# A Trainium2 kernel's convolution backward with its complex products summed before one inverse matmul each, and with its opening, gradient stores, load chain and shift-kernel gradient rearranged

## The chip, the cores and the metric

The kernel runs on one core of one Trainium2 chip, in bf16 with float32 accumulation. A core has five engines, each with its own instruction stream: TensorE (PE in the profile; its weight loads are listed apart as PEld), VectorE (DVE), ScalarE (ACT), GpSimd (POOL) and SyncE (SP). They meet only through semaphores. Here SP and POOL serve above all as queues that issue DMA transfers: what is issued on one of them leaves in order. The metric is device microseconds of one execution, taken as the median over several runs.

## The reference

The kernel computes the forward pass and all gradients of a four-step residual network over a sequence of 2048 positions with 448 channels. The hidden width of the dense part is 1792.

```python
def _A_ref(q, k, v, shift_k, ssm_k, ssm_D):
    k_shift = sum over t of k_pad[:, t:t + S, :] * shift_k[:, ks - 1 - t]     # 4 taps
    kv = k_shift * v
    y_f = rfft(kv padded to 2 S) * rfft(ssm_k padded to 2 S)
    y = irfft(y_f)[:S] + kv * ssm_D
    return q * y

def _B_ref(x, w1, w2):
    return silu(x @ w1) @ w2

x = A_q
x = x + _A_ref(_layernorm(x), A_k, A_v, A_shift_k, A_ssm_k, A_ssm_D)
x = x + _B_ref(_layernorm(x), B_w1, B_w2)
x = x + _A_ref(_layernorm(x), A_k, A_v, A_shift_k, A_ssm_k, A_ssm_D)
x = x + _B_ref(_layernorm(x), B_w1, B_w2)
out, vjp = jax.vjp(all of the above, ...); grads = vjp(grad_out)
```

(The 4-tap sum is shortened here to one line.) Two layers share all weights. The part A of a layer multiplies the normalized input by y, which does not depend on x, so y is computed once and serves both layers. Nine results leave: the output and the gradients of A_q, A_k, A_v, A_shift_k, A_ssm_k, A_ssm_D, B_w1 and B_w2.

## The kernel before

**Three sections, one stream of matmuls.** `_ssm_prefix` computes y: the shift convolution, the long convolution as a Fourier transform in two matmul stages (first stage L207, a turn by TensorE L348, second stage L218), the products with the kernel's spectrum (L449 and L450), the inverse of the second stage (L227 and L228) and of the first (L467). It leaves both spectra in DRAM (`SPEC_d`, L156). `Main.run` (L689) does both layers, forward and backward. `_ssm_suffix` (L1023) takes the gradient of y back through the convolution. The order of instructions on TensorE in the last two sections is the one in which the program emits them (L189). The other engines' instructions are placed by the framework's scheduler, and DMAs go out in the order of their queue, SP or POOL.

**Main.** The sequence is cut into 4 chunks of 512 positions (index c), each passing through layers L = 0 and 1. `fwd0` and `fwd1` do the part A of a layer: layer norm (`_ln`, L253, whose scaled copy is L274) and the gate (L549) on VectorE. `T` transposes a [128, 4, 448] tile by TensorE in two steps of 8 transposes (`transp`, L513; ScalarE copies each out of PSUM). `H` (7 steps of 8 matmuls, L597) multiplies by w1; ScalarE makes `aT` by silu and later the slope `dT` (L612). `O` (8 half steps, L619) multiplies by w2 and VectorE adds to the residual `X` (L623). On the way back `G` (7 steps, L638) multiplies the turned gradient by w2 transposed, and `N` (8 half steps, L665) by w1 transposed, followed by the layer norm's backward on VectorE (`_ln_bwd`). Where the program interleaves, a string gives the order of the steps, one letter a step. It does so in the opening, before the loop over chunks:

```python
        weave("TTGGGGtGtGG", T=self.T(k.gb0, gT, GBLK), G=self.G(gT, gh2), t=self.T(self.n0[0][1], nT, NBLK))
...
        weave("OOOOOOTOTO", O=self.O(0, 0, aT), T=self.T(gb1, gT, GBLK))
```

There the G steps of layer 1 (they need only `grad_out`, as `gb0` for chunk 0 and `gb1` for chunk 1) stand between the forward steps. `gb1` is loaded on POOL's queue (L715), and `w1T` comes by a transposing DMA on SP's queue (L486).

**Weight gradients.** The gradients of w1 and w2 need, for each of 14 blocks of 128 hidden channels, a sum over all 2048 positions of both layers: products of `a` (the silu outputs) or `g` (gradients times slope) with full-length tiles `X`, `go`, `n1m`, `n3m`. `store` (L496) writes `a` and `g` to DRAM (`OP_d`). For a of both layers and g of layer 1 it first turns each half by two transposing DMAs into a buffer and stores that by two more; g of layer 0 is stored as it is, and turned by the load (L873). `Jobs` (L813) is the stream of these matmuls: `load` (L861) brings a block into a `dstat` tile, `mms` (L876) does 16 matmuls of 448 columns in steps of four, and `jobs.run(n)` puts the next n steps at the place in TensorE's order where it is called; `jobs.run(1000)` at the end does what is left. After the main section (`pool is None`) every second `dstat` tile comes from the `hd` buffers (L195), which the main section used for `x0c` and `n00`, and the others from three buffers that held slopes.

**The convolution's backward.** First stage of the gradient of y (L1043), turned by TensorE (L1068) into 7 tiles `Zg`. Then, for each of 7 passes (cp): `spectrum` (L1078) does the second stage of the next tile and has VectorE write `xsw`, the tile with its real and imaginary halves exchanged (L1088); `inverse` (L1091) multiplies the tile by two stored spectra, that of kv for the gradient of the long kernel and that of the long kernel for the gradient of kv, and transforms back. In a chunk of 1024 columns it does this for each of the two: VectorE makes `pa` = tile x spectrum and `pb` = exchanged tile x spectrum, and 16 matmuls (8 with each, two different constant matrices of `Gsb`) add them up in PSUM as `ps_v`, 28 times in all; then 3 steps of jobs. After each pass VectorE does an eighth of the part A backward of layer 0 (`APart.run`, L1004), with loads and a store on POOL's queue. `spec_load` (L1056) brings both spectra for a pass by two DMAs of 512 KB; two buffers (`kk_c`, `kk_d`) alternate.

**The end.** gkv (L1142) gives the gradients of v and of the shifted k (`gks`), gK (L1162) the long kernel's. The shift kernel's gradient is the diagonal of a [channel x channel] product for each of four taps: for each of four blocks of 112 channels, 16 matmuls with 4 x 112 columns into `ps_sk` (L1174), of which VectorE keeps the diagonal by multiplying with the identity (`skjunk`, L1177). The gradient of k is formed on VectorE alone in 16 groups (L1186 to L1189), the last part stored from POOL's queue. The rest of the jobs follows.

## Time and profile before

| what | value |
|---|---|
| median of 3 runs | 779.42 us (769.31, 779.42, 792.57) |
| profiled execution, own time | 767.89 us |
| its span, first to last instruction | 765.8 us |
| mean granted TensorE clock | 0.988 |

Busy time by stretch of the span, from the windows view:

| stretch (us) | what runs there | PE | DVE | ACT | DMA share |
|---|---|---|---|---|---|
| 0 to 101 | prefix | 84.2 | 73.0 | 75.1 | 0.81 |
| 101 to 164 | opening of the main section | 50.1 | 32.3 | 40.0 | 1.12 |
| 164 to 541 | main section | 364.2 | 228.6 | 250.4 | 0.70 |
| 541 to 575 | first stage of the backward, and jobs | 33.5 | 10.8 | 21.1 | 0.96 |
| 575 to 680 | turn and 7 passes of products and inverse, and jobs | 104.7 | 76.9 | 51.3 | 1.02 |
| 680 to 715 | gkv and gK, and jobs | 33.0 | 27.5 | 16.8 | 0.98 |
| 715 to 766 | shift kernel's gradient, gradient of k, last jobs | 46.6 | 26.9 | 4.3 | 0.62 |

How to read the lines that follow: a row of the timeline or of the chain is start, duration, engine, line, operation, output <- inputs, shape, type and count; in square brackets stands the idle time of that engine before it, and what released it. L879 means line 879 of the kernel as printed above. Busy time of TensorE counts matmuls whose ends are modelled, and pipelined matmuls overlap, so the pace of a run of matmuls is read from the starts of neighbouring runs rather than from the mean duration of one. The granted clock is TensorE's, 1.00 being full speed.

### The profile page before, as it was taken

The page shows a single profiled execution, that of the slowest core. Times are in us where ns is not written, and L with a number is a line of the kernel's source. Part 1 is how long each engine was busy: PE and PEld are TensorE (multiplying, and loading weights), DVE is VectorE, ACT ScalarE, POOL GpSimd, SP SyncE. Part 2 cuts the span into 40 slices and gives each one's busy share as a digit, 9 for nine tenths or more (in the row PEclk, how much of TensorE's full clock was granted, in tenths as well). Part 3 has the DMA queues.
Part 4 walks back from the last instruction along what each step waited for, and adds up shares of the span by engine and source line. Part 5 has one row for each costly group of instructions (what it writes and reads, how often), then busy time and mean ns, then how long its engine had stood idle before and what let it go on. Part 6 is the DMA issues. An engine that isn't in the chain of part 4 may idle for free.

```text
span 765.8 us, 12392 instructions
## 1 busy us (share of the span) xinstructions
PE 716.3 (94%) x4831; PEld 403.5 (53%) x4860; DVE 476.0 (62%) x1148; ACT 458.9 (60%) x579; POOL 125.5 (16%) x209
## 2 busy tenths in 40 slices
PE   6998789779999999999999999999799999989997
PEld 4976544335444444544445544544366666656653
DVE  4789841664686747866379524825058777659970
ACT  4878867668776877769677793133465445445200
POOL 1134310120011100111001000000312323242311
PEclk9999999989999999999999999999899999999999
DMA  9949799989963898149882597185999999889972
GB/s 320 261 150 293 274 154 118 224 224 224 212 157 133 197 253 221 61 140 208 213 189 76 156 232 289 29 238 169 358 258 296 253 337 287 229 268 383 218 183 78
DMA packets 186363, 163.91 MB, mean 214 GB/s; under 512 B 135490, under 2 KB 166338, under 8 KB 185152
## 3 DMA queue, kind: packets, MB, share of 16 engines
q1 hardware_dynamic: 171776, 106.61, 57.9%
q0 software_dynamic: 14064, 56.50, 22.7%
q8 instruction: 38, 0.62, 0.3%
q14 instruction: 21, 0.17, 0.1%
q10 hardware_dynamic: 464, 0.00, 0.0%
HBM read 66.18 MB, written 60.10 MB: 165 GB/s over the span
## 4 chain that ended last, share of the span: by engine, by line
PE 61%; ACT 12%; DMA 9%; issue 8%; DVE 7%; POOL 3%; POOLq 0%; SPq 0%; DVEq 0%; ACTq 0%
PE ps_d L879 11%; PE ps_h L597 11%; PE ps_n L665 10%; PE ps_g L638 9%; PE ps_o L619 6%; ACT dT L612 4%; DMA out_dram<-gK 2%; DMA kx_s<-in_A_k_dram 2%; PE ps_d L914 2%; PE ps_t L520 2%; PE ps_s L207 2%; PE ps_v L228 2%; PE ps_v L227 2%; ACT aT L600 1%; ACT nT L521 1%
## 5 line engine op out<-in xcount | busy, mean ns | idle before, releaser
L879 PEld LDWEIGHTS <-dstat 128*128 128x128 bf16 x800 | 76.6, 99 | 70.6 <-DMA dstat<-a_d 4.6
L597 PE MATMUL ps_h<-nT,w1sb 112*128 112x512 bf16 x448 | 104.5, 379 | 4.2 <-ACT dT L111 1.9
L638 PE MATMUL ps_g<-nT,w2T 128*128 128x512 bf16 x432 | 101.0, 384 | 1.5 <-ACT nT L521 0.7
L665 PE MATMUL ps_n<-w1T,ghT 128*128 128x448 bf16 x448 | 95.3, 353 | 1.8 <-DVE ghT L650 1.7
L619 PE MATMUL ps_o<-w2sb,aT 128*128 128x448 bf16 x448 | 88.8, 352 | 0.0
L648 ACT CAST ghT<-ps_g 128x1024 bf16<-128x1024 f32 (+1 forms) x68 | 54.5, 824 | 52.5 <-PE ps_g L638 51.0
L600 ACT ACTIVATE aT<-ps_h 128x1024 bf16<-128x1024 f32 (+1 forms) x72 | 58.4, 834 | 30.5 <-PE ps_h L597 29.8
L597 PEld LDWEIGHTS <-w1sb 112*128 112x128 bf16 x448 | 43.7, 98 | 57.0 <-issue 7.5
L638 PEld LDWEIGHTS <-w2T 128*128 128x128 bf16 x448 | 44.0, 99 | 51.7 <-issue 1.6
L805 DVE SCALAR_TENSOR_TENSOR lb_v<-lb_u,n 128x448 bf16<-128x448 bf16 x48 | 29.9, 624 | 64.0 <-ACT lb_u L669 63.6
L665 PEld LDWEIGHTS <-ghT 128*128 128x128 bf16 x448 | 43.2, 98 | 44.3 <-DVE ghT L650 4.0
L619 PEld LDWEIGHTS <-aT 128*128 128x128 bf16 x448 | 43.4, 98 | 39.8
L612 ACT ACTIVATE dT<-dT 128x1024 bf16<-128x1024 bf16 (+1 forms) x64 | 54.6, 935 | 0.1
L267 POOL TENSOR_TENSOR rstd<-ln_ve,mhalf 128x2 f32<-128x2 f32 (+1 forms) x25 | 22.3, 890 | 187.6 <-DVE ln_ve L265 186.8
L111 ACT CAST dT<-ps_h 128x1024 bf16<-128x1024 f32 (+1 forms) x59 | 52.2, 902 | 0.0
L879 PE MATMUL ps_d<-n1m,dstat 128*128 128x448 bf16 x224 | 48.5, 356 | 0.1
L521 ACT COPY nT<-ps_t 128x1024 bf16<-128x1024 bf16 (+1 forms) x32 | 32.3, 1010 | 27.0 <-PE ps_t L520 27.0
L879 PE MATMUL ps_d<-n3m,dstat 128*128 128x448 bf16 x224 | 48.2, 352 | 0.2
L227 PE MATMUL ps_v<-Gsb,pa 128*128 128x128 bf16 x336 | 43.0, 219 | 3.1 <-DVE pa L449 3.0
L228 PE MATMUL ps_v<-Gsb,pb 128*128 128x128 bf16 x336 | 42.2, 219 | 2.3 <-DVE pb L450 1.9
L879 PE MATMUL ps_d<-X,dstat 128*128 128x448 bf16 x176 | 39.7, 366 | 4.2 <-DMA dstat<-a_d 4.2
L669 ACT ACTIVATE lb_u<-ps_n,rstd 128x448 bf16<-128x448 f32 x32 | 20.6, 645 | 32.2 <-PE ps_n L665 18.1
(197 smaller groups left out, 1201.2 us busy)
## 6 DMA issues: line engine op xcount, KB each, us to landing
dstat<-a_d SPq DMA_DIRECT2D x26, 512.0 KB, 5.7
a_d<-turned SPq DMA_DIRECT2D x16, 512.0 KB, 4.0
g_d<-ghT SPq DMA_DIRECT2D x8, 896.0 KB, 4.4
dstat<-g_d SPq DMA_DIRECT2D x14, 512.0 KB, 5.8
a_d<-turned SPq DMA_DIRECT2D x16, 384.0 KB, 3.2
N_d<-n POOLq DMA_DIRECT2D x11, 448.0 KB, 5.0
g_d<-turned SPq DMA_DIRECT2D x8, 512.0 KB, 3.4
spec_K<-Z POOLq DMA_DIRECT2D x7, 512.0 KB, 7.3
```

The lines of the kernel that those rows point to most:

```text
L111: nc.scalar.copy(out, in_)
L227: nc.tensor.matmul(pv[:, i, :], lhsT=pa[:, i * P:(i + 1) * P], rhs=k.Gsb[:, ga, :], start=True, stop=False)
L228: nc.tensor.matmul(pv[:, i, :], lhsT=pb[:, i * P:(i + 1) * P], rhs=k.Gsb[:, gb, :], start=False, stop=True)
L521: nc.scalar.copy(dst[:rows, 2 * h:2 * h + 2, :], pt[:rows])
L597: nc.tensor.matmul(ps[:, u, :], lhsT=self.w1sb[:, dc, ft * P:(ft + 1) * P], rhs=nT[:DC, dc, :], start=(dc == 0), stop=(dc == ND - 1))
L600: self.last_silu = nc.scalar.activation(aT[hh][:, o:o + hi - lo, :], ps[:, lo:hi, :], ACT.Silu)
L612: self.nc.scalar.activation(d[:, o:o + n, :], d[:, o:o + n, :], ACT.Derivative_silu)
L619: nc.tensor.matmul(po[:, :D], lhsT=aT[ft // 7][:, ft % 7, tl * P:(tl + 1) * P], rhs=self.w2sb[:, ft, :], start=(ft == 0), stop=(ft == NF - 1))
L638: nc.tensor.matmul(ps[:, u, :], lhsT=self.w2T[:, b, ft * P:(ft + 1) * P], rhs=gT[:, b, :], start=(b == 0), stop=(b == ND - 1))
L648: nc.scalar.copy(g, ps[:, lo:hi, :])
L665: nc.tensor.matmul(pn[:, :D], lhsT=gh[ft // 7][:, ft % 7, tl * P:(tl + 1) * P], rhs=self.w1T[:, ft, :], start=(ft == 0), stop=(ft == NF - 1))
L879: self.nc.tensor.matmul(ps[:, :D], lhsT=st[:, t, :], rhs=mov[:, t, :], start=(first and t == 0), stop=(last and t == NT - 1))
```

## The change

- **Products.** VectorE makes `q` = tile x spectrum and `q2` = exchanged tile x spectrum, and adds them into `q`; one matmul per 128 columns with one combined matrix (`GiQ`, `G_IQ`) follows, 8 per chunk and spectrum in place of 16. The sign that the second product needs is put into the exchanged tile: the second half of `_swap_halves` is a multiplication by -1 instead of a copy. The copies out of PSUM always go to ScalarE; before, a balance chose between ScalarE and VectorE. `jobs.run(3)` becomes `jobs.run(4)`.
- **Spectra.** Both lie in one DRAM tile by chunk. `spec_load` brings one chunk of 1024 columns of both spectra by two DMAs of 512 KB, and each buffer now holds the real half (64 rows) twice, in partitions 0 to 63 and 64 to 127, and beside it the imaginary half twice: 28 such DMAs for 14 chunks in place of 14 for 7 passes. A load is issued after each chunk. The buffers stay two.
- **Gradient turned on its way out.** g of layer 0 is turned before its store like the other three, and all loads of `dstat` are plain.
- **Chain.** Each load of `dstat` is placed behind the one before it, and the `hd` buffers serve for `dstat` only from the fourth load on.
- **Opening.** The gate and layer norm of chunk 0 are emitted pair by pair of token groups, the layer norm of `fwd1(0)` by groups 0-2, 2-3 and 3-4, and the transposes of both results go by the same three groups into three PSUM banks (`T2`). Three G steps of chunk 0 come before H and the other four after O; the transposes of `gb1` come after O's first half step; the slope waits for the copy out of the last of them.
- **Bands.** The shift kernel's gradient is formed in bands of 32 channels: 224 matmuls of 4 x 32 columns in place of 64 of 4 x 112, all into one PSUM bank; VectorE takes the diagonals by two masked products, two reductions and eight small copies. `skjunk` shares the buffer of `gka` with the groups of the gradient of k. One `jobs.run(4)` follows, in place of four times `jobs.run(1)`.
- **Smaller.** The part A backward has three buffers for its gradient in place of two; two tiles of the prefix change places in memory; `_ln` stores only the groups it was given.

```diff
-    GiAc, GiBc = inv_pair(True)
-    GiBc = np.roll(GiBc, 64, axis=0)
-    Gs = np.stack([G, GiA, GiB, GiAc, GiBc], axis=1)
+    GiA = build(lambda ci, co: (1.0, -1.0)[ci] * (Ct if co == 0 else St))
+    GiB = build(lambda ci, co: -St if co == 0 else Ct)
+    GiQ = build(lambda ci, co: (Ct, -St)[ci] if co == 0 else (St, Ct)[ci])
+    Gs = np.stack([G, GiA, GiB, GiQ], axis=1)
...
-    k.TURNED = {("a", 0), ("a", 1), ("g", 1)}
...
 def _swap_halves(k, dst, src):
     k.nc.vector.tensor_copy(dst[0:64], src[64:128])
-    return k.nc.vector.tensor_copy(dst[64:128], src[0:64])
+    return k.nc.vector.tensor_scalar(out=dst[64:128], in0=src[0:64], scalar1=-1.0, scalar2=None, op0=ALU.mult)
...
     def store(self, key, tile_, c, hh):
         nc, k = self.nc, self.k
         dst = k.OP_d[key]
-        if key not in k.TURNED:
-            nc.sync.dma_start(out=dst[7 * hh:7 * hh + 7, :, 512 * c:512 * (c + 1)].rearrange("ft f s -> f ft s"), in_=tile_[:])
-            return
         prev = None
         for lo, hi in ((0, 4), (4, 7)):
...
+            n01 = self.t([P, 4, D], "n01", bufs=2)
+            for g in ((0, 2), (2, 4)):
+                self.gate(0, lambda tl: xc[:, tl, :], n00, (g,))
+                _ln(k, self.ch, 0, self.xs(0), 1, n01, (g,))
+            self.n0[c] = (n00, n01)
+            return
...
-        pairs = ((0, 2), (2, 4))
+        pairs = ((0, 2), (2, 4)) if c else ((0, 2), (2, 3), (3, 4))
...
+    def slope(self, dT, behind=None):
+        with self.tc.issue_after((behind or self.last_silu).ins):
...
+    def T2(self, src, dst, blocks):
+        nc, k = self.nc, self.k
+        rows = max(hi - lo for lo, hi in blocks)
+        for lo, hi, tag, bufs in ((0, 2, "tr", 1), (2, 3, "jb", 1), (3, 4, "po", 2)):
+            pt = k.psum.tile([P, ND, 256], BF16, name="ps_t", tag=tag, bufs=bufs)
+            for i, (b0, b1) in enumerate(blocks):
+                for tl in range(lo, hi):
+                    nc.tensor.transpose(pt[:rows, i, (tl - lo) * P:(tl - lo + 1) * P], src[:, tl, b0:b1], k.ident[:])
+            nc.scalar.copy(dst[:rows, :, lo * P:hi * P], pt[:rows, :, 0:(hi - lo) * P])
+            yield
...
-        nT, gT = self.nT(), self.nT()
+        gT, nT = self.nT(), self.nT()
         gh2 = []
-        weave("TTGGGGtGtGG", T=self.T(k.gb0, gT, GBLK), G=self.G(gT, gh2), t=self.T(self.n0[0][1], nT, NBLK))
+        g20 = self.G(gT, gh2)
+        def steps(pattern, **gens):
+            for ch in pattern:
+                next(gens[ch], None)
+        steps("TTTGGtGttt", T=self.T(k.gb0, gT, GBLK), G=g20, t=self.T2(self.n0[0][1], nT, NBLK))
         gb1 = _hd(k, [P, 4, D], "gb1")
         nc.gpsimd.dma_start(out=gb1[:], in_=_pm(k.grad_out[0])[:, 4:8, :])
         gb = gb_load(0)
         weave("H" * 7, H=self.H(0, 0, nT, r, (1, 3, 5)))
         aT, dT1 = r
         gT = self.nT()
-        self.slope(dT1)
-        weave("OOOOOOTOTO", O=self.O(0, 0, aT), T=self.T(gb1, gT, GBLK))
+        o = self.O(0, 0, aT)
+        steps("OTOTT", O=o, T=self.T(gb1, gT, GBLK))
+        self.slope(dT1, self.last_copy)
+        weave("O" * 6, O=o)
         self.fwd1(0)
-        nT = self.nT()
 
         gh21 = []
         g21 = self.G(gT, gh21)
-        tn = self.T(self.n1[1], nT, NBLK)
-        for g in (g21, g21, tn, g21, tn):
-            next(g)
+        steps("GGGG", G=g20)
+        next(g20, None)
+        nT = self.nT()
+        steps("tGtGtGt", G=g21, t=self.T2(self.n1[1], nT, NBLK))
...
-        if self.pool is None and i % 2:
+        if self.pool is None and i % 2 and i > 3:
             st = _hd(k, [P, NT, P], "dstat")
         else:
             st = k.dp3.tile([P, NT, P], BF16, name="dstat", tag="dstat", bufs=3)
         src = k.OP_d[key]
-        if key in k.TURNED:
-            nc.sync.dma_start(out=st[:], in_=src[:, ft, :, :])
-        else:
-            nc.sync.dma_start_transpose(out=st[:], in_=src[ft, :, :])
+        with ExitStack() as es:
+            if self.last_ld is not None:
+                es.enter_context(k.tc.issue_after(self.last_ld.ins))
+            self.last_ld = nc.sync.dma_start(out=st[:], in_=src[:, ft, :, :])
         return st
...
+            def spec_load(ci):
+                kk = (kk0 if ci == 0 else kk1 if ci == 1 else sp.tile([P, 2, 2, 1024], BF16, name="kk_c", tag="kk0") if ci % 2 == 0
+                      else p1.tile([P, 2, 2, 1024], BF16, name="kk_d", tag="kk1"))
+                for h in (0, 64):
+                    nc.gpsimd.dma_start(out=kk[h:h + 64].rearrange("p c m n -> p c (m n)"), in_=k.SPEC_d[:, ci].rearrange("(c p) m n -> p c (m n)", c=2))
                 return kk
...
-            def inverse(cp, t):
+                return xsw
+            def inverse(cp, xsw):
                 for u in range(2):
                     ci = 2 * cp + u
                     o = slice(u * 1024, (u + 1) * 1024)
-                    for spec_t, B1, cnd in ((t[1], B1k, True), (t[0], B1v_, False)):
-                        pa = p1.tile([P, 1024], BF16, name="pa", tag="pab", bufs=5)
-                        pb = p1.tile([P, 1024], BF16, name="pb", tag="pab", bufs=5)
-                        nc.vector.tensor_tensor(out=pa[:], in0=Zf[cp][:, o], in1=spec_t[:, o], op=ALU.mult)
-                        last = nc.vector.tensor_tensor(out=pb[:], in0=t[2][:, o], in1=spec_t[:, o], op=ALU.mult)
-                        bal.add("dve", 2.2)
-                        _fft_inv_stage2_chunk(k, pa, pb, True, B1, ci, psum, cnd=cnd)
-                        jobs.run(3)
+                    for m in (1, 0):
+                        q = p1.tile([P, 1024], BF16, name="q", tag="pab", bufs=4)
+                        q2 = p1.tile([P, 1024], BF16, name="q2", tag="pab", bufs=4)
+                        nc.vector.tensor_tensor(out=q[:], in0=Zf[cp][:, o], in1=kks[ci][:, 0, m, :], op=ALU.mult)
+                        nc.vector.tensor_tensor(out=q2[:], in0=xsw[:, o], in1=kks[ci][:, 1, m, :], op=ALU.mult)
+                        last = nc.vector.tensor_tensor(out=q[:], in0=q[:], in1=q2[:], op=ALU.add)
+                        pv = psum.tile([P, 8, P], FP32, name="ps_v", **mm)
+                        for i in range(8):
+                            nc.tensor.matmul(pv[:, i, :], lhsT=q[:, i * P:(i + 1) * P], rhs=k.Gsb[:, G_IQ, :], start=True, stop=True)
+                        if m:
+                            nc.scalar.copy(B1k[:, :, 32 * ci:32 * ci + 32].rearrange("p q (dh ds) -> p dh q ds", ds=4), pv[:].rearrange("p dh (q ds) -> p dh q ds", ds=4))
+                        else:
+                            nc.scalar.copy(B1v_[:, 8 * ci:8 * ci + 8, :].rearrange("p a b -> p (a b)"), pv[:].rearrange("p a b -> p (a b)"))
+                        jobs.run(4)
+                    if ci + 2 < NCI:
+                        kks.append(spec_load(ci + 2))
                 return last
...
-        gsk = p2.tile([DC, ND, 4], FP32, name="gsk")
-        for dc in range(ND):
-            pd = psum.tile([P, 4, P], FP32, name="ps_sk", **mm)
+        mask = p2.tile([P, 32], FP32, name="skmask")
+        for b in range(0, P, 32):
+            nc.vector.tensor_copy(mask[b:b + 32, :], k.ident[b:b + 32, b:b + 32])
+        pd = psum.tile([P, 2, 512], FP32, name="ps_sk", **mm)
+        for r0 in range(4):
+            bands = 4 if r0 < 3 else 2
             for sl_ in range(16):
-                nc.tensor.matmul(pd[:DC, :, :DC], lhsT=gks[:, sl_, dc * DC:(dc + 1) * DC], rhs=kx[:, sl_:sl_ + 4, dc * DC:(dc + 1) * DC], start=(sl_ == 0), stop=(sl_ == 15))
+                for b in range(bands):
+                    ch = slice(P * r0 + 32 * b, P * r0 + 32 * b + 32)
+                    nc.tensor.matmul(pd[32 * b:32 * b + 32, 0, P * r0:P * r0 + P], lhsT=gks[:, sl_, ch], rhs=kx[:, sl_:sl_ + 4, ch], start=(sl_ == 0), stop=(sl_ == 15))
+        junk = p2.tile([P, 4, 4, 32], FP32, name="skjunk", tag="gka")
+        gsk = p2.tile([P, 4, 4], FP32, name="gsk")
+        gskb = p2.tile([P, 4, 4], BF16, name="gskb")
+        for n, lo, hi in ((P, 0, 3), (64, 3, 4)):
+            nc.vector.tensor_tensor(out=junk[:n, lo:hi], in0=pd[:n, 0, P * lo:P * hi].rearrange("p (r u c) -> p r u c", u=4, c=32), in1=mask[:n].rearrange("p (a b c) -> p a b c", a=1, b=1).to_broadcast([n, hi - lo, 4, 32]), op=ALU.mult)
+            nc.vector.tensor_reduce(out=gsk[:n, lo:hi], in_=junk[:n, lo:hi], op=ALU.add, axis=mybir.AxisListType.X)
             for j in range(4):
-                junk = p2.tile([DC, DC], BF16, name="skjunk", tag="skjunk", bufs=2)
-                nc.vector.scalar_tensor_tensor(out=junk[:], in0=pd[:DC, 3 - j, :DC], scalar=1.0, in1=k.ident[:DC, :DC], op0=ALU.mult, op1=ALU.mult, accum_out=gsk[:, dc, j:j + 1])
-            jobs.run(1)
-        gskb = p2.tile([DC, ND, 4], BF16, name="gskb")
-        nc.vector.tensor_copy(gskb[:], gsk[:])
+                nc.vector.tensor_copy(gskb[:n, lo:hi, j], gsk[:n, lo:hi, 3 - j])
+        jobs.run(4)
...
-        s_ = p2.tile([P, 2, D], FP32, name="gka")
+            nc.gpsimd.dma_start(out=k.outs[4][0:384].rearrange("(r p) j -> p r j", p=P), in_=gskb[:, 0:3, :])
+            nc.gpsimd.dma_start(out=k.outs[4][384:448], in_=gskb[:64, 3, :])
+        s_ = p2.tile([P, 2, D], FP32, name="gka", tag="gka")
```

## The prediction

> **What bounds the kernel now.** I read the page's engine shares first, then the chain of waits, then TensorE's timeline where the chain has holes, then VectorE's at the end. Times are us from the span's start.
>
> ```profile
> PE 716.3 (94%) x4831; PEld 403.5 (53%) x4860; DVE 476.0 (62%) x1148; ACT 458.9 (60%) x579; POOL 125.5 (16%) x209
> ...
> 673.70 0.22 PE L228 MATMUL ps_v<-Gsb,pb 128*128 128x128 bf16 x1
> 673.75 2.43 PE L879 MATMUL ps_d<-n1m,dstat 128*128 128x448 bf16 x12
> 676.02 0.22 PE L227 MATMUL ps_v<-Gsb,pa 128*128 128x128 bf16 x1
> ...
> 715.28 3.19 PE L1174 MATMUL ps_sk<-kx_s,gks 128*112 128x448 bf16 x16
> 718.31 0.92 PE L879 MATMUL ps_d<-go,dstat 128*128 128x448 bf16 x4
> ...
> 758.44 3.19 PE L879 MATMUL ps_d<-X,dstat 128*128 128x448 bf16 x16
> ```
>
> TensorE is the bound nearly everywhere: 128-column matmuls start 0.0555 apart, 448-column ones 0.189 apart (12 in 2.27, from 673.75 to 676.02), and the weight-gradient matmuls at L879 fill every gap and end the span. The holes are few. Two matter here:
>
> ```profile
> 145.73 0.62 DVE L623 TENSOR_TENSOR X<-X,ps_o 128x448 bf16<-128x448 bf16 x1 [1.90 <-PE ps_o L619]
> ...
> 152.50 0.57 PE L520 MATMUL ps_t<-ident,n 128*112 128x128 bf16 x2 [3.36 <-DVE n L274]
> ...
> 155.64 1.09 PE L520 MATMUL ps_t<-ident,n 128*112 128x128 bf16 x6 [2.56 <-DVE n L274]
> ```
> ```profile
> 540.88 1.67 PE L879 MATMUL ps_d<-X,dstat 128*128 128x448 bf16 x4 [4.16 <-DMA dstat<-a_d]
> 542.35 0.95 PE L207 MATMUL ps_s<-Ysb,M1h 128*128 128x448 bf16 x2
> ...
> 546.91 0.92 PE L879 MATMUL ps_d<-X,dstat 128*128 128x448 bf16 x4
> ```
>
> After each hole the matmuls go at half rate for 4 to 5 us: four take 1.47 at 540.88 (to 542.35), 0.76 in the undisturbed run at 718.31. So a hole costs its length and some 2.5 more.
>
> **The change, part by part.** Sums are against the profiled execution (767.89, span 765.8). The median of the runs shown is 779.42, 1.5% above it; I scale by 1.015 at the end.
>
> *Inverse products.* A chunk had 16 matmuls, now 8: 28 x 8 x 0.0555 = **-12.4** on the path.
>
> *Filler.* `jobs.run(3)` becomes 4 in 28 chunks: 28 x 4 x 0.189 = **+21.2** before the inverse ends, and as much less after the bands. That would be neutral if TensorE ended the kernel; the tail decides (below).
>
> *VectorE in that stage.* A pass of 4 chunks costs it 12 products at 0.605 (start to start, L1098/L1099), two half swaps at 0.70 and the A part at 4.75: 13.4, or 14.0 if the negating swap goes at the rate of the scaled copy at L274 (448 in 0.39). TensorE's pass is 4 x (0.445 + 3.03) + 2.4 + 0.2 = 16.5. So the sums hide behind TensorE; without that cover each excess us would cost 7.
>
> *Spectrum loads.* Both halves are loaded twice: 28 issues of 512 KB instead of 14, two buffers of one chunk pair. A buffer freed by the last product on it is wanted again 8.4 to 11.5 later (A part 4.75 plus two chunks of 1.8, up to TensorE's slower pace). Loads landed in 6.5 and 7.3 in the median, 11.7 at worst, and in the built order a wait for ScalarE stands between the two halves on POOL's queue. I take **+3** (0 to 12). Bandwidth as such is no worse: the transposing loads of g_d0 go away (575 to 615 shows a DMA share of 1.09 at only 278 GB/s; 541 to 575, with few of them, 0.96 at 322).
>
> *Gradient turned on its way out.* Loads of g_d never made TensorE wait, so plain ones gain nothing. The stores get two transposes and two writes per half on SP's queue, some 18 per chunk by the neighbouring stores (366.4 to 385), against 7. Behind them stand the stores of aT and x0c, which start at most 3 later; VectorE and TensorE need x0c some 5 later still. 0, up to +3. The scan's loads n3m and n1m change places; n3m had about 3 to spare and now lands behind 1.8 MB more: **+1** (0 to 3).
>
> *The dstat chain.* The 540.88 load used a buffer held until the main part's VectorE work ended near 536. It now takes a buffer that TensorE frees; the one that still waits (a_d1, block 6) is wanted two blocks later, after 8 steps of 1.14 us, and lands at 541 as before. So 4.2 of hole and 2.6 of slow clock go: **-6.8** (-4 to -7). Late next would be block 5, needed at 541, landing about 538.
>
> *The opening.* Three G steps instead of seven come before H, so H starts near 113.9 and ends at 127.5; the other four fill the hole at 148 to 156. But the transposes of gb1, which stood behind O's first six steps, now come after the first, at 129.0, and TensorE is in order. Their load:
>
> ```profile
> 101.25 38.39 SPq L486 DMA_TRANSPOSE w1T<-in_B_w_dram  x1
> ...
> L715 POOL DMA_DIRECT2D gb<-in_grad_out_dram x1: 675/675/675, 107.2 to 107.2; - x1
> ...
> DMA to landing us min/median/max: 29.6/29.6/29.6
> ```
>
> It crawls beside the turning of w1T and lands at 136.8; before, nobody asked for it until 140.4. The change alters neither load, so TensorE stands 7.9, then runs slow (+2.4). From there: transposes and O 10.2, end near 149.5; four G steps 6.9; layer norm chain as before (first n 7.4 after the last O); H at 163.7 against an equivalent 161.7 (175.4, when O starts, less 13.7). **+2** (-1 to +4); with gb1 on time it would be -7.7.
>
> *gkv.* TensorE's 2-us hole at 687 waited for gks, whose load stood behind the A part's last store on POOL. VectorE now runs up to two chunks ahead, so that store leaves earlier: **-3.9** with the slow clock (0 to -4).
>
> *Bands and the tail.* 64 matmuls of 448 columns (4 x 3.03 = 12.1) become 224 of 128 columns on 32-column weights. No row shows such ones. At the pace of 128-column ones 224 make 12.4; above, if each weight load (0.098) stood alone, 22; below, four bands side by side, 3.1. I take 9, nearer to the 128-column row, since each band still loads its own weights.
>
> The Trainium skill (TensorE: Matmul & The Clock Gate, Part 3) says column tiles do run together, three of them 2.38 times faster at 512 columns, but also that weight loads overlap running matmuls only in another row group, which these bands do not have; by the first the bands would take about 5.2 (an estimate from that page), by the second they stay near 12. No run here shows it.
>
> What matters more is who waits. The masked read-out uses the buffer tag of `gka`, and in the built order VectorE has it ahead of the 16 gk groups, two L1186 products apart. Before, those groups ran from 695 on, under TensorE:
>
> ```profile
> 713.40 1.08 DVE L1186 TENSOR_TENSOR B1v<-gks,skx 128x1792 bf16<-128x1792 bf16 x1
> ...
> 716.06 1.08 DVE L1186 TENSOR_TENSOR B1v<-gks,skx 128x1792 bf16<-128x1792 bf16 x1
> ...
> 746.82 0.62 DVE L1189 TENSOR_TENSOR B1v<-gka 128x448 bf16<-128x448 f32 x1
> ```
>
> A group takes 2.67. Now all come after the bands: read-out 3.0 (two PSUM products between the rows of 0.27 for 112 and 0.61 for 448 elements, two reductions alike, eight 0.15 copies partly overlapped), 16 x 2.67 - 2 = 40.7, last store 4.2 (0.9 to issue, 3.3 as at the end now): 47.9. TensorE has only 17 steps, 12.9, left by then. So VectorE ends the kernel, the filler moved forward is really paid, and from the start of the bands it takes 9 + 47.9 = 56.9 against 50.5 (715.3 to 765.8): **+6.4** (0.5 to 19).
>
> Sum: -12.4 + 21.2 + 3 + 1 - 6.8 + 2 - 3.9 + 6.4 = **+10.5**. So 778.4 profiled, times 1.015: 790.
>
> **Rivals.**
> 1. *Slower by over 2%: late spectrum reloads.* Place: the two buffers in the inverse. It decides once a reload takes over about 9 us from release to landing; then VectorE, in order, stops the A part and the next products with it, and TensorE with only two chunks of lead. Twelve reloads late by 1.5 each add 18 in place of 3: +25.5, 805. For: landings up to 11.7, the ScalarE wait between halves. Against: medians near 7, fewer tiny packets.
> 2. *Faster by over 2%: the two new waits do not bite.* gb1 lands by 129 (-9.7) and gk runs under TensorE as before (-16: its last store landed about 72 after gkv's start, and now 31.4 + 56.9 = 88). +10.5 - 25.7 = -15: 764. Against: the built order on both engines forbids the second, the 38-us transpose the first.
> 3. *The complex sum does not shorten TensorE's path at all*, because VectorE turns out the slower of the two per pass. At 16.5 against 14.0 it needs 2.5 more per pass; then 7 x 2 = +14 on top, again slower.
>
> **How the numbers follow.** A run of this kernel tells about 2% from no change (769 to 793 for the same kernel): 764 to 795 counts as same. The forecast, 790, has 0.55; the slow cases (1 and 3) 0.36; the fast one 0.09. Low: no reload waits (-3), bands at 3.1 (-5.9), no n3m (-1), the opening at its low end (-3) give -2.4, and a gb1 that lands 3 earlier still -5.4: 773. High: reloads at 12 (+9), bands at 12.4 (+3.4), the opening at +4 (+2) give +25: 805. That range leaves out about two in ten.
>
> **What would show it.** Right: no wait of TensorE for dstat<-a_d near 536; a wait of ps_t for DMA gb of 5 to 9 us near 130; ps_v in runs of 8, passes of 16.5; TensorE idle for the last 25 to 30 us while L1217, L1218 and L1220 run to the end. Wrong: no wait for gb, the bands under 4 or over 16 us, kk_c or kk_d among the longest waits of VectorE, or the last instruction on TensorE.

## The result, and the profile after

The changed kernel takes 819.88 us in the median of four runs (816.60 to 821.70). Its time is 1.061 times that of the kernel before, 95% interval 1.057 to 1.066. Two of the four runs of the kernel before, taken beside it, were in a slower state of the chip and are left out of this ratio. It is slower, where 790 (773 to 805) and "no change" had been forecast. The profiled execution took 818.81, its span 817.0, against 767.89 and 765.8. Where the 51.2 of span went, by the starts of TensorE's stages:

| stretch, by its ends | before | after | difference | forecast |
|---|---|---|---|---|
| start to the backward's first stage | 532.8 | 525.9 | -6.9 | +2 |
| first stage to the turn | 27.0 | 21.2 | -5.8 | -6.8 |
| turn to the first n3m job | 10.8 | 24.1 | +13.3 | +1 |
| first n3m job to gkv (the 7 passes) | 108.8 | 150.6 | +41.8 | +11.8 |
| gkv to the shift kernel's gradient | 35.9 | 31.5 | -4.4 | -3.9 |
| from there to the end | 50.5 | 63.7 | +13.2 | +6.4 |

The first line of the page, the page's DMA issues (size, median time to landing), and the longest waits of TensorE and of VectorE (total, times, longest):

```profile
PE 705.7 (86%) x4767; PEld 392.0 (48%) x4796; DVE 496.5 (61%) x1165; ACT 459.0 (56%) x581; POOL 140.2 (17%) x227
...
kk_c<-spec POOLq DMA_DIRECT2D x14, 512.0 KB, 10.5
kk_d<-spec POOLq DMA_DIRECT2D x14, 512.0 KB, 13.2
```
```profile
PE ps_v L1118 <- DVE q L1115: 14.3, 7, 4.5
PE ps_d L895 <- DMA n3m<-N_d: 13.1, 1, 13.1
PE ps_sk L1201 <- issue: 8.5, 5, 3.2
PE ps_d L895 <- DMA go<-in_grad_out_dram: 7.3, 1, 7.3
```
```profile
DVE q L1113 <- DMA kk_d<-spec: 26.2, 6, 7.2
...
DVE q L1113 <- DMA kk_c<-spec: 15.7, 6, 5.2
```

TensorE has 10.6 less work, and its busy share has gone from 94% to 86%. Of its four long waits two end with a DMA, and that of ps_v does so through VectorE, which waits 41.9 for reloaded spectra (`kk_c`, `kk_d`). Those land after 10.5 and 13.2 in the median, where before the medians were 6.3 to 8.1. The wait for dstat near 536 is gone, as forecast; the wait for gb that was forecast did not come.

The windows view of the long stretch, after and before (window and length, busy time and count of PE, PEld, DVE, ACT and POOL, then granted clock, DMA share, GB/s):

```profile
571.20:721.80 150.60, 128.43 (x810) 71.93 (x816) 97.00 (x211) 56.61 (x71) 40.66 (x67) 0.92 0.98 280
```
```profile
570.60:679.40 108.80, 108.42 (x914) 69.19 (x918) 80.24 (x187) 54.62 (x67) 29.48 (x52) 1.00 1.03 270
```

The 16 DMA engines were full before, too (share 1.03), but TensorE was busy for all of the 108.8, so it did not show. Now 42.1 MB came through in place of 29.4, and the engines' share is 0.98 for all of the 150.6, while TensorE's own work is 108.8 - 12.4 + 21.2 = 117.6. VectorE (97.0 busy) is not full. The clock of 0.92 is another loss, by estimate 8% of 150.6, or 12. It goes with the waits, as in this row at the start of the stretch, where four matmuls take 1.44 (to 572.65) in place of 0.76:

```profile
571.21 1.65 PE L895 MATMUL ps_d<-n3m,dstat 128*128 128x448 bf16 x4 [13.11 <-DMA n3m<-N_d]
```

The end, in TensorE's timeline and VectorE's:

```profile
753.26 1.41 PE L1201 MATMUL ps_sk<-kx_s,gks 128*32 128x128 bf16 x86
755.92 1.26 PE L1201 MATMUL ps_sk<-kx_s,gks 128*32 128x128 bf16 x46 [1.25 <-issue]
...
763.55 0.31 PE L1201 MATMUL ps_sk<-kx_s,gks 128*32 128x128 bf16 x3 [3.17 <-issue]
766.97 2.66 PE L1201 MATMUL ps_sk<-kx_s,gks 128*32 128x128 bf16 x62 [3.12 <-issue]
```
```profile
769.67 0.75 DVE L1206 TENSOR_TENSOR skjunk<-ps_sk,skmask 128x384 f32<-128x384 f32 x2 [18.22 <-PE ps_sk L1201]
...
810.56 1.09 DVE L1218 TENSOR_TENSOR gka<-B1v 128x896 f32<-128x896 bf16 x1
811.68 0.63 DVE L1220 TENSOR_TENSOR B1v<-gka 128x448 bf16<-128x448 f32 x1
```

Where the bands run, 86 matmuls take 1.41, 0.0164 each; then TensorE starts nothing for 3 at a time ("issue": nothing that the profile shows released it). VectorE starts its read-out only after the last of them and works to 812; TensorE's last matmul starts at 782.4. So the bands took 16.0 from the first start to the last, and the tail behind them 47.7 (769.3 to 817.0).

### The profile page after: what moved, and what is told of

Its sections match the earlier page's. It is cut to its first block, busy times and chain, and to the rows that moved or that the text cites. A ratio compares the mean times of both kernels' runs of the same rounds, so it can differ in the third digit from the quotient of the medians.

```text
span 817.0 us, 12343 instructions
## 1 busy us (share of the span) xinstructions
PE 705.7 (86%) x4767; PEld 392.0 (48%) x4796; DVE 496.5 (61%) x1165; ACT 459.0 (56%) x581; POOL 140.2 (17%) x227
## 4 chain that ended last, share of the span: by engine, by line
PE 47%; DMA 18%; issue 13%; ACT 11%; DVE 8%; POOL 4%; POOLq 0%; SPq 0%; ACTq 0%; DVEq 0%
PE ps_h L592 10%; PE ps_n L660 9%; PE ps_g L633 8%; PE ps_o L614 6%; DMA kk_d<-spec 5%; PE ps_d L895 4%; DMA n3m<-N_d 3%; ACT dT L607 3%; DMA kk_c<-spec 2%; PE ps_d L930 2%; DMA KB<-Z 2%; DMA go<-in_grad_out_dram 2%; DMA kx_s<-in_A_k_dram 2%; PE ps_s L199 2%; PE ps_t L506 1%
## 5 line engine op out<-in xcount | busy, mean ns | idle before, releaser
L595 ACT ACTIVATE aT<-ps_h 128x1024 bf16<-128x1024 f32 (+1 forms) x72 | 58.4, 834 | 31.6 <-PE ps_h L592 30.9
L895 PE MATMUL ps_d<-n3m,dstat 128*128 128x448 bf16 x224 | 50.4, 368 | 13.4 <-DMA n3m<-N_d 13.1
L255 POOL TENSOR_TENSOR rstd<-ln_ve,mhalf 128x2 f32<-128x2 f32 (+2 forms) x27 | 23.0, 852 | 182.4 <-DVE ln_ve L253 181.6
L895 PE MATMUL ps_d<-go,dstat 128*128 128x448 bf16 x176 | 41.0, 369 | 7.3 <-DMA go<-in_grad_out_dram 7.3
L507 ACT COPY nT<-ps_t 128x1024 bf16<-128x1024 bf16 (+1 forms) x28 | 28.3, 1012 | 20.8 <-PE ps_t L506 20.8
L1120 ACT CAST A1g<-ps_v 128x1024 bf16<-128x1024 f32 x14 | 14.2, 1012 | 33.9 <-PE ps_v L1118 33.9
## 6 DMA issues: line engine op xcount, KB each, us to landing
dstat<-g_d SPq DMA_DIRECT2D x28, 512.0 KB, 10.6
kk_c<-spec POOLq DMA_DIRECT2D x14, 512.0 KB, 10.5
kk_d<-spec POOLq DMA_DIRECT2D x14, 512.0 KB, 13.2
```

The lines of the kernel that those rows point to most:

```text
L255: nc.gpsimd.tensor_tensor(out=r[:, lo:hi], in0=ve[:, 0:n], in1=k.mhalf[:, 0:n], op=ALU.pow)
L507: self.last_copy = nc.scalar.copy(dst[:rows, 2 * h:2 * h + 2, :], pt[:rows])
L595: self.last_silu = nc.scalar.activation(aT[hh][:, o:o + hi - lo, :], ps[:, lo:hi, :], ACT.Silu)
L895: self.nc.tensor.matmul(ps[:, :D], lhsT=st[:, t, :], rhs=mov[:, t, :], start=(first and t == 0), stop=(last and t == NT - 1))
```

## The experiments

Each diff shows the lines that matter, without line numbers; the rest of the edit is left out. "The stretch" is the one from the first n3m job to gkv, 150.6 in the changed kernel. A profiled span is given beside each median.

**Old products.** The changed kernel with the products and spectra as before; the diff gives the loops in short form.

```diff
-                    for m in (1, 0): q, q2, q += q2; 8 matmuls with G_IQ; jobs.run(4)
+                    for spec_t, B1, cnd in (...): pa, pb; 16 matmuls; jobs.run(3)
```


> The changed kernel with the complex products, the spectrum layout and loads, the three job steps per chunk and the two part A buffers as before; opening, dstat chain, turned g0 and bands stay. In the changed kernel the stretch from the first n3m job (571.2) to the first gkv matmul (721.8) takes 150.6, before 108.8. Theory A (the doubled spectrum bytes load the 16 DMA engines beyond what they move, share 0.98): that stretch falls to 105 to 115 and the wait for n3m, 13.1 in the changed kernel, falls under 5 since half a MB less is in front of it; total some 770 to 782 profiled. Rival B (the stretch is long because the opening's gain only brings it earlier onto the same transfers): the stretch stays above 125, and the total above 790.

Measured: 773.08, ratio to before 1.0025 (0.9986 to 1.0063); span 767.6, stretch 110.3, TensorE's wait for n3m 3.6. Of the 51.2 lost, 49.4 go with this part, in which products, spectra and filler are taken back together; what is still lost at the end (bands and tail) and won at the front about cancel. The DMA share in the stretch is 0.78, against 1.03 in the kernel before: the plain loads of g did free the room that the prediction counted on.

**Half the spectrum bytes.** The kernel leaves out the second spectrum DMA from the third chunk on, so four of its gradients are not the reference's.

```diff
-                for h in (0, 64):
+                for h in (0, 64)[:2 if ci < 2 else 1]:
```


> The changed kernel with the second of the two spectrum DMAs left out from the third chunk on, into two fixed buffers: 12 x 512 KB = 6.3 MB less, the other 64 partitions keep the values of the first two chunks, so the gradients of ssm_k, A_k, A_v and shift_k are not the reference's. Number and order of the operations on TensorE and VectorE are unchanged. Theory A (DMA engines full, some 280 GB/s in that stretch): 6.3 MB are worth 22; the stretch 571 to 722 shrinks by 18 to 26, total 793 to 801. Rival C (the two buffers look ahead too little, whatever the bytes): a reload of half the size still starts when VectorE has done the chunk and lands in 7 to 10 instead of 13, the stretch shrinks by 8 to 14.

Measured: 798.21, ratio 1.032 (1.020 to 1.043) to the kernel before; span 799.3 (17.7 less than the changed kernel), stretch 123.2 (27.4 less):

```profile
572.40:695.60 123.20, 119.63 (x811) 68.98 (x817) 95.36 (x215) 56.36 (x71) 30.98 (x51) 0.98 0.93 290
```

TensorE's wait of ps_v for VectorE's products is 1.3 in place of 14.3. All operations of the compute engines are still there, so it is the loads that cost.

**More look-ahead.**

```diff
-                    if ci + 2 < NCI:
-                        kks.append(spec_load(ci + 2))
+                        if ci + 2 < NCI:
+                            kk_ = spec_load(ci + 2, m)
```


> The changed kernel with the same spectrum bytes in twice as many DMAs of 256 KB, each issued as soon as the product on its half buffer is done, so a reload has three product steps in place of two until it is wanted (some 12 in place of 8). Theory A (DMA engines full): the same bytes take the same time, total within 4 of the changed kernel's 818.8, and the waits of VectorE for kk stay near their sum of 26. Rival C (too little look-ahead): landings of 10 to 13 are now in time, the waits for kk fall under 8 and the total to 795 to 803.

Measured: 822.23, span 821.6, stretch 144.6, ps_v still waits 10.6. VectorE still waits 30.9 for spectra (41.9 in the changed kernel), and DMAs of half the size land after 9.8 and 13.1, as late as the whole ones. Earlier issue buys 6 in the stretch and nothing in total: too little look-ahead is not the main cause.

**Spectra once, sum from halves.** The spectrum bytes of before, in loads of all 128 partitions by pass, and one VectorE operation more per product.

```diff
-                        last = nc.vector.tensor_tensor(out=q[:], in0=q[:], in1=q2[:], op=ALU.add)
+                        nc.vector.tensor_tensor(out=q[0:64], in0=q[0:64], in1=q[64:128], op=ALU.add)
+                        last = nc.vector.tensor_tensor(out=q[64:128], in0=q2[0:64], in1=q2[64:128], op=ALU.add)
```


> The changed kernel with the spectra loaded once, by pass, as before (7.3 MB less), and the complex sum made by VectorE from halves: q and q2 are products with the plain spectrum, then one addition of the two halves of q and one of the two halves of q2, 64 partitions each; 4 VectorE operations per chunk and spectrum in place of 3, on TensorE all is as in the changed kernel. Theory A (the doubled bytes are the price): the stretch from the first n3m job to gkv, 150.6 in the changed kernel, falls to 115 to 125 although VectorE does 28 more operations of 0.6, total 785 to 797. Rival R (the products on VectorE hold TensorE back in themselves): VectorE's pass becomes 15.8 of TensorE's 16.5 and the stretch stays above 135, total above 803.

Measured: 795.83, ratio 1.031 (1.024 to 1.039); span 794.5; the stretch in the windows view:

```profile
565.90:690.70 124.80, 121.41 (x816) 69.59 (x816) 115.86 (x234) 56.25 (x71) 29.08 (x48) 0.97 0.81 275
```

124.8 with 18.9 more work on VectorE than in the changed kernel; the DMA share has gone from 0.98 to 0.81. The doubled loads were the price. They cost in two ways. In the packets' records 34.3 MB took 101.1 of the 16 engines' time here, 340 GB/s; at that pace the 42.1 MB of the changed kernel would take 124, and they took 147.6. So of the 46.5 more some 23 are the bytes, and the other 24 are slower packets: in the stretch those of 4 KB on the spectra's queue took 268 ns in the changed kernel and 278 with half of the loads left out, but 181 here and 200 in the kernel before, where the engines were fuller (1.03). So fullness does not explain them. They go with loads that write only 64 of the 128 partitions: a run below that brings each row once, but by 64 partitions (the copies on the chip), has 236. Why is open. VectorE, at 116 of 125, is the next in line.

**n3m first, small store late.** Two edits, each read in its own stretch.

```diff
+            with k.tc.issue_after(self.n3_ld.ins):
                 k.nc.sync.dma_start(out=self.n1t[:], in_=_pm(k.N_d[1][:]))
...
+        with tc.issue_after(gsk_i.ins):
+                nc.gpsimd.dma_start(out=k.outs[6].rearrange("(c p) -> p c", p=DC), in_=gKD[:])
```


> The changed kernel with two edits in different places, each read in its own stretch: the load of n1m is put behind that of n3m (before, n3m went first), and the 2-byte-wide store of the gradient of ssm_D goes behind the bands in place of just ahead of them. First edit, theory A (the transfers themselves are the limit from 526 on): n3m lands some 6 earlier, since 1.8 MB fewer are ahead of it, and TensorE's wait of 13.1 shrinks to 6 to 9, but what it gains is mostly given back in the stretch up to 722. Rival F (the swap of the two loads is the cause): the wait falls under 3 as in the kernel before. Second edit, theory G (in the bands, 7 of the 16 are TensorE without code: the records show one 16 KB instruction transfer of 8.8 at 757 among 4 KB writes of 2 to 6.5, and the bands run 86 matmuls in 1.41 where they run): with the tiny store gone the writes are short and the bands take 4 to 8. Rival H (the tiny store is not what slows the writes): the bands stay at 14 to 18.

Measured: 806.89, ratio 1.038 (1.026 to 1.049); span 802.8. The wait for n3m fell from 13.1 to 7.8, not under 3: the order of the two loads is 5.3 of it. With the order of the changed kernel it is 3.6 with the old products and 5.1 with the sum from halves, so 8 to 9.5 go with how the spectra are loaded. (The two do not simply add.) As many bytes of spectra, 2 MB, are issued ahead of n3m in all of these; from the first stage to the first n3m job the 4 KB packets on their queue take 260 ns in the changed kernel and 164 and 165 in those two runs, and n3m lands after 25.0, against 15.5 and 17.0. The bands:

```profile
745.41 2.97 PE L1200 MATMUL ps_sk<-kx_s,gks 128*32 128x128 bf16 x196
750.50 0.96 PE L1200 MATMUL ps_sk<-kx_s,gks 128*32 128x128 bf16 x28 [2.12 <-issue]
```

5.8 in place of 16.0. In the seven runs with bands and this store just ahead of them, the bands take 11.1 (old products) and 15.5 to 18.1 (the others); in the five with the store behind them, or in rows, 5.6 to 6.6. So the store's place is shown. How it holds TensorE is argued only. The records of the queue that brings instructions have a transfer of 16 KB in the bands: 8.8 long in the changed kernel, 10.5 in the run with the sum from halves, 0.9 here, which suggests code that comes behind the store's writes. But with half the spectrum bytes and with the gradient of k first (below) these transfers took 3.1 and 1.0, and TensorE still stood 12.8 and 12.5 in all. The 448 writes of 2 bytes themselves are no quicker (landed after 18.1 here, 18.0 in the kernel before).

**Gradient of k first.** The 16 groups emitted ahead of the bands.

```diff
+        for g in range(16):  # the groups of the gradient of k, moved here
         pd = psum.tile([P, 2, 512], FP32, name="ps_sk", **mm)
...
-        for g in range(16):
```


> The changed kernel with the 16 groups of the gradient of k emitted ahead of the bands, nothing else. Theory D (the last 35 are VectorE's 16 groups of 2.67 behind the bands' read-out, TensorE done at 782.4): the groups start when gkv's products and the shifted rows are there, run beside gK, the bands and the last jobs, and the end falls to 785 to 793 (TensorE's end, or the groups' end plus read-out and store). Rival E (the rows that the groups need come so late that they start after the bands anyway): less than 8 gained.

Measured: 792.46, ratio 1.024 (1.014 to 1.035); span 793.0, 24 less: TensorE's last matmul is at 784, VectorE's last operation at 781. So most of the tail came from VectorE's order.

**Places, opening, dstat.** Three one-part kernels around the opening, one for the dstat buffers.

```diff
-        A1kv = spec.tile([P, NDH, 2, 16, 4], BF16, name="A1kv")
         A1K = spec.tile([P, NDH, 2, 16, 4], BF16, name="A1K")
+        A1kv = spec.tile([P, NDH, 2, 16, 4], BF16, name="A1kv")
```


> The changed kernel with the two tiles of the prefix in their former places. Theory K (their place decides when and beside what w1T is turned): the transposing load of w1T takes 35 to 40 again (18.2 in the changed kernel), gb1 lands past 130 and TensorE waits 5 to 8 for it near 129, as was forecast. Rival L (the 38 of the one profiled execution of the kernel before were an accident of that execution): the load takes 17 to 21 and nobody waits for gb1.

Measured: 819.12; w1T took 25.8 and nobody waited for gb1.

The other way round, in the kernel before:

> The kernel before with the two tiles of the prefix in their new places, nothing else. The transposing load of w1T took 38.4 and 34.7 in two kernels with the former places and the former opening, 25.8 with the former places and the new opening, 17.7 to 20.5 with both new. Theory S (the places decide): 18 to 26 here. Rival T (the order of the opening decides): 33 to 40. No more than 2 of the total in either case, since nobody waits for w1T or gb1 in this opening.

Measured: 772.64, ratio 0.997 (0.992 to 1.003); w1T took 18.0.

The opening alone, in the kernel before with its places:

> The kernel before with the opening of the change (groups, step order, slope behind the copy, partial stores of the layer norm) and the former places. Theory T (the order of the opening decides): w1T turns in 18 to 27, gb1 is there, and the first stage of the backward starts at 525 to 529 in place of 532.8. Rival S (the places decide): w1T takes 33 to 40 and TensorE waits 5 to 8 for gb1 near 129.

Measured: 774.16, ratio 1.000 (0.994 to 1.005); w1T took 41.4, and TensorE shows the wait that was forecast for the change:

```profile
127.26 1.49 PE L629 MATMUL ps_o<-w2sb,aT 128*128 128x448 bf16 x7
139.94 1.04 PE L521 MATMUL ps_t<-ident,gb 128*128 128x128 bf16 x8 [11.20 <-DMA gb<-in_grad_out_dram]
```

(ps_t waits for gb in the second row.) So in the kernel before the two tiles' places decide: 38.4, 34.7 (the next run) and 41.4 with the old ones, 18.0 with the new. In the changed kernel the old ones give 25.8, in between, so they are not all of it. The order of the opening does not shorten the load.

The dstat buffers alone, in the kernel before:

```diff
-        if self.pool is None and i % 2:
+        if self.pool is None and i % 2 and i > 3:
```


> The kernel before with one edit: the hd buffers serve for dstat only from the fourth load on. Theory M (the 4.2 of TensorE at 536 and the slow clock after it come from that buffer): no wait for dstat<-a_d there, the first stage of the backward starts 4 and the turn 5 to 7 earlier than in the kernel before (559.8), total 761 to 765 profiled. Rival N (the next block's load is late instead): a wait of 3 or more for another dstat between 530 and 560. Its w1T load also shows whether 38 comes back in a kernel with the former places (rival L of the run on the places: 17 to 21).

Measured: 777.65, ratio 0.999 (0.993 to 1.004). First stage to turn is 21.2, as in the change, 5.8 less than before, and no wait for dstat is left; but the stretch is 114.7 in place of 108.8. So the whole is the same within its interval: what was gained here was lost again in the stretch.

**Versions.** Old products, n3m first, gradient of k first, small store behind the bands:

> The changed kernel with the products, spectra and three job steps of before (as in the run with the old products), n3m ahead of n1m, the gradient of k ahead of the bands and the tiny store behind them. If the transfers of the doubled spectra, VectorE's late groups and the code stall in the bands are the three costs, TensorE ends the span again, with the opening's 6, the dstat chain's 6 and some 6 of the bands gained on the kernel before: 745 to 755, at least 12 under the kernel before. If not, it stays above 760.

Measured: 758.51, ratio 0.975 (0.967 to 0.982). Its last matmul starts at 749.0, yet the span is 759.9: ScalarE's output copies wait 17.4 for a store, and the small store on the same queue landed after 18.8. With that store turned into rows:

```diff
+        nc.tensor.transpose(pkd[:], gKD[:], k.ident[:DC, :DC])
+        nc.scalar.copy(gKT[:], pkd[:])
+        nc.gpsimd.dma_start(out=k.outs[6].rearrange("(c p) -> c p", p=DC), in_=gKT[:])
```


> The version of the last run (758.5: old products, n3m first, gradient of k ahead of the bands) with the gradient of ssm_D turned by one small TensorE transpose and stored as 4 rows of 224 bytes in place of 448 elements of 2 bytes. Theory P (its last 7 us are ScalarE's copies waiting 17 for output stores that stand behind the element-wise store, which took 18.8 to land): the end follows the last matmul by 4 to 6 in place of 11, total 750 to 755. Rival Q (the tail has another cause): within 3 of 758.5.

Measured: 753.50 (752.23 to 756.65), ratio 0.974 (0.965 to 0.983): the lowest time of the study, below the kernel before; whether by more than 2% is open. Against the version above the ratio does not tell (0.975 and 0.974), but the small store lands after 4.0, and the end follows TensorE's last matmul by 6.4 in place of 10.9. Its page begins:

```profile
span 751.3 us, 12752 instructions
...
PE 704.1 (94%) x4992; PEld 398.4 (53%) x5021; DVE 475.8 (63%) x1137; ACT 459.3 (61%) x582; POOL 127.1 (17%) x213
```

Two tries at keeping the new products:

> The changed kernel's products (8 matmuls, sum on VectorE, four job steps) with each spectrum half loaded once and copied on the chip into the other 64 partitions, one half by VectorE, one by ScalarE, per chunk; n3m first, gradient of k ahead of the bands, gradient of ssm_D stored in rows. Theory A (the bytes were the price of the products): the 7.3 MB less bring TensorE's path back, the 12.4 of matmuls saved show: 738 to 748, or up to 752 if VectorE's 14 copies of 0.7 lie on its path. Rival R (VectorE and the two-buffer look-ahead hold the products back even with the bytes of before): waits of ps_v for q stay at 10 or more, total above 756.

Measured: 777.10, ratio 1.008 (1.003 to 1.013). It settles nothing on the products: the copies stand in VectorE's and ScalarE's fixed order and wait there for loads, ScalarE's first one for 12.1 in the first stage, where TensorE then stood 12.7; the stretch is 138.6.

> The same with n3m ahead of n1m, the gradient of k ahead of the bands and the gradient of ssm_D stored in rows. If theory A holds and VectorE's 15.8 per pass stay hidden, this is the version with the old products (753.5) less the 12.4 of matmuls: 741 to 750. If VectorE's passes are on the path (rival R): 753 to 765.

Measured: 758.33, ratio 0.982 (0.976 to 0.988). The stretch is 127.0 with VectorE busy for 118; by TensorE's work it would be 117.5 (108.7 in the version above, -12.4 and +21.2). With the bytes gone, 9.5 of the 12.4 that the matmuls give are lost again; with VectorE that busy it is the likely limit, which no run shows by itself. No version shows a gain of the new products: 0.982 with them, 0.974 without, and the intervals overlap.

## Why the prediction was wrong

- **Products and filler (-12.4, +21.2):** their sum roughly fits. With fewer bytes the stretch is 123 to 125, against 117.6.
- **Spectrum reloads (+3, 0 to 12): the step that failed.** The text said that "Bandwidth as such is no worse: the transposing loads of g_d0 go away". In the records of the stretch those loads had 44 of the 112 of engine time, and they did go; but plain loads replaced them, with the doubled spectra and the 7 tiles of the filler there were 12.7 MB more to move, and the packets of 2 to 4 KB on the queue of the spectra slowed from 184 to 249 ns. The stretch is bound by the sum of its transfers, and the term measured +41.8 - 8.8 = 33, beyond its upper bound of 12 (TensorE's wait of 7.3 for go is in it). That bound came from how late one reload can be, not from the bytes of all.
- **Rival 1** (late reloads, 805) had the place and the sign: its condition, a reload over about 9, held (10.5 and 13.2), and so did the chain from reload to VectorE to TensorE. It put 18 on the reloads, and they measured 33. What it did not have is why they are late: issued earlier they gain 6, with half of them left out 27. **Rival 2** came true in its first half (gb1 on time), not in its second. **Rival 3** did not: VectorE is busy 97.0 in 7 passes, 13.9 each, as forecast.
- **n3m (+1, 0 to 3) measured +13.3.** Taken as a swap of two loads; undoing it takes 5.3 off the wait. Loading the spectra as before takes off 8 to 9.5, though the stages ahead stay as short. So n3m, asked for at 558 in a window whose DMA share is 0.97, is late mostly because of the loads of the spectra in their new shape.
- **dstat (-6.8):** right, -5.8, in the change and alone.
- **Opening (+2, -1 to +4) measured -6.9.** The step "the change alters neither load" failed: w1T was turned in 18.2 and gb1 landed after 9.1. The change of places, which the prediction had not costed, does that in the kernel before. With w1T slow, the forecast wait appears (11.2 for 7.9); for a gb1 on time the prediction's own figure was -7.7, near the -6.9. In the changed kernel the old places give 25.8, and still nobody waits, so another part of the change shortens the load too; which one is open.
- **gkv (-3.9):** right, -4.4: the loads of gks now start 0.1 before gkv in place of 1.8 after it, and no hole is left.
- **Bands (9; 3.1 to 22) measured 16.0,** in two parts that the prediction did not have: the bands start near its lower end, 0.0164 a matmul (3.7 for all), and TensorE then stands 8.5 without a releaser, which goes with the small store ahead; some 4 are slower matmuls around these gaps. So 9 was neither part. Of the two rules that the prediction cites from the Trainium skill (TensorE: Matmul & The Clock Gate, Part 3), the one on column tiles agrees with this trace (3.7 against the estimate of 5.2). The one on weight loads does not: 86 loads of some 97 ns each lay in 1.23, so they overlapped.
- **VectorE's tail (47.9):** right, 47.7, with the cause as forecast.
- **The factor 1.015** on the sum has nothing behind it here: the changed kernel's median (819.88) lies 0.1% above its profiled execution. So the sum (778.4) was 40 too low, of which 30 are the seven passes, 12 n3m and 7 the bands, less 9 won at the front.

## What to carry to other kernels

Bound a change's transfers by the bytes of the whole stretch over the rate that the stretch shows, next to TensorE's work there (here 42.1 MB at the 270 GB/s of before, 156, against 117.6); and do not take the rate for fixed when the shape of the loads changes. A full DMA share that costs nothing today is the price of the next byte, and of any time saved ahead of it. When a read-out shares a buffer with a long chain on an in-order engine, count the chain as waiting for it. Look for stores of a few bytes per element ahead of long runs of short instructions: placed behind them, this one took the bands from 16.0 to 5.8.

## What was not expected of the hardware

- 448 writes of 2 bytes took 17 to 19 to land, the same numbers as 4 rows 4.0, and a 16 KB instruction transfer just behind them 8.8 to 10.8 in four runs (in two others 1.0 and 3.1) instead of about 1.
- The Trainium skill (Runtime: NRT & Kernel Launch, Instruction fetch mechanics) says that code comes in blocks of 16 KiB and that crossing one is mostly hidden. In these bands, 448 short instructions with that store ahead, TensorE stood 7 to 13 with no releaser shown; if that was code, it was not hidden here.
- Matmuls on 32-column weights in four bands went as if side by side: 0.0164 from start to start with a weight load each, against 0.0555 for those on 128-column weights, so that 224 would take 3.7.
- Loads of the spectra that write 64 partitions each had 4 KB packets of 236 to 278 ns on their queue in the stretch, also where each row was brought only once (236); loads of all 128 partitions 176 to 200.
- A transposing load took 18 or 38 with two other tiles' places exchanged: 17.7 to 20.5 in the twelve runs with the new places, 25.8 to 41.4 in the four with the old ones. Why stays open.
